# Spreading 1/rms through DRAM instead of with selector matmuls, in an attention and channel-mix kernel

The change replaces, for batches 3 to 7, the matmuls that spread the reciprocal rms over the partitions by a write to DRAM and a broadcast read. With it comes a new order of every instruction, made so that transposes and loads are apart in time, and finer stores at the end.

## Chip, cores and metric

One core of a Trainium2 chip. The metric is device time in microseconds (us) of one execution, lower is better. A profile is one execution seen by the hardware profiler; its span, from first to last instruction, is 1.7 to 2.5 us shorter than the time of that run. Engines are named as the profile names them: PE (TensorE), PEld (its weight loads), DVE (VectorE), ACT (ScalarE), POOL (GpSimd), SP (SyncE). "SPq" and "ACTq" are those two engines' sequencers, where transfers are issued.

## The reference, cut to what matters

```python
# q, k, v: (8 batches, 8 heads, 576 rows, 64) float32
kv  = einsum('bhsd,bhse->bhde', k, v)
out = einsum('bhsd,bhde->bhse', q, kv)
rms = sqrt(mean(out * out, axis=-1, keepdims=True) + 1e-06)
x   = out / rms * g_norm                      # then heads side by side: (8, 576, 512)

x_prev = x shifted by one row, zero first
xk = mu_k * x + (1 - mu_k) * x_prev
xr = mu_r * x + (1 - mu_r) * x_prev
k  = maximum(xk @ w_k, 0)                     # 512 -> 1024
r  = sigmoid(xr @ w_r)                        # 512 -> 512
result = r * ((k * k) @ w_v)                  # 1024 -> 512
```

The attention part goes by batch (576 rows), the mix by groups of 512 rows: nine groups, 0 to 8. A group needs `x` of one or two batches; group 3 is the first that needs batch 3, group 4 needs 3 and 4, group 5 needs 5 after the end of 4.

## The kernel before

The program is a set of pieces, each for one engine, and a hand-made list `ORDER` that says in which order all pieces are emitted. Each engine runs its own instructions strictly in that order. An entry is `name:engine:slots`; a slot is a buffer of the kind that the piece claims. PSUM is the kind `ps` with only four slots (2 x 512 float32 on each partition), and a piece that claims a slot waits until the last user of that slot is done.

Names, with batch `b` or group `g`: `load_*` loads (issued by POOL); `qTd` transpose by DMA (issued by SP); `kv`, `u` the two attention products on small PE tiles; `kvc`, `uc` their copies out of PSUM; `sq` squares; `st` sum of squares on PE; `rs` the reciprocal square root on ACT; `sp` its spread by PE; `x` the multiply; `d` difference to the row before; `tk`, `tr`, `xk`, `xr` the blends; `K`, `relu`, `sqk`, `R`, `sig`, `V`, `o` the mix; `S` its stores, issued by SP.

The step that the change replaces, for batches 1 to 7. `rs` has one row per head pair and head in use, so each row has to be spread over 64 partitions:

```python
st = add(f"st{b}", {"PE": 0.25}, st_mm, deps=sqs + [p_ones], bufs=[pst, sq], mode=3)
rp = add(f"rs{b}", {"ACT": 0.54}, st_rs, deps=[st], bufs=[pst, rs], mode="norm")
for half in range(2):
    pp = [Buf("ps") for _ in range(2)]                       # two PSUM slots

    def sp_mm(_, half, pp):                                  # line 530 is its matmul
        for hp in range(NHP):
            nc.tensor.matmul(get(pp[hp // 2])[:, hp % 2, 0:HS], sel[32 * hp:32 * hp + 32].rearrange("p e d -> p (e d)"),
                             get(rs)[32 * hp:32 * hp + 32, HS * half:HS * half + HS], start=True, stop=True)

    def x_mul(_, half, i, ps):                               # line 535; g_norm is inside sel
        c = HS * half
        nc.vector.tensor_tensor(out=get(xT)[:, 2 * i:2 * i + 2, NP + c:NP + c + HS],
                                in0=flat(slice(2 * i, 2 * i + 2))[:, :, c:c + HS], in1=get(ps)[:, :, 0:HS], op=ALU.mult)
# ... cut ...
```

The stores, in pieces that follow the layout of the output (one piece may be two or more transfers):

```python
def store(eng, g, ci, ot, cs):
    row = 0
    while row < 128:
        # ... cut: the next run of rows that lie together ...
        (nc.sync if eng == "SP" else nc.scalar).dma_start(out=dst, in_=ot[row:row + cnt, cs])
        row += cnt
```

The order around batch 3, cut to it (`st3` to its first blend):

```
st3::3 rs3::0 kvc4.0.0:D:0 kvc4.0.2:D kvc4.0.1:D R2.0::2 relu2.1::1 sp3.0::03 load_q6.0::1 sqk2.3 R2.1 R2.3::1
x3.0.1::1 x3.0.0 sqk2.1 sig2.0::1 sp3.1::30 S1.0 x3.1.0 R2.2 sig2.1::2 x3.1.1 d3.0::0 d3.2 S0.0 tk3.2:D:0 xk3.2
```

## Time and profile before

| | before |
|---|---|
| time, median of 3 runs | 210.9 us (210.78 to 212.5) |
| span of the profiled run | 207.6 us |
| PE, DVE, ACT busy | 94%, 68%, 59% |
| first R, first K (the start of its weight load; its first matmul is 0.2 us later) | 19.3 us, 24.5 us |
| first K to the end of the last matmul | 176.4 us |
| last matmul to the end | 6.7 us |

Below are the head of the profile page and its rows for PE and for the clock. The rows cut the span into 40 slices of 5.2 us; a digit is the busy share in tenths, in the row PEclk the granted TensorE clock in tenths of full speed.

```profile
span 207.6 us, 3798 instructions
## 1 busy us (share of the span) xinstructions
PE 195.7 (94%) x1526; PEld 93.9 (45%) x1526; DVE 141.1 (68%) x262; ACT 122.0 (59%) x146; POOL 28.7 (14%) x45
## 2 busy tenths in 40 slices
PE   7598999999999999999999999999999999999970
...
PEclk9955999999999999999999999999999999999998
```

PE is full from the fifth slice to the last but two: this kernel is bound by PE's work, but for its start (half clock in two slices) and its tail. The chain that ended last, by engine, says the same:

```profile
PE 88%; DMA 3%; ACT 2%; POOL 2%; DVE 1%; issue 1%; POOLq 0%
```

The timeline around batch 3 shows the spread. Columns: start in us, duration, engine, line, operation, output and input, count, and in brackets the idle time before it and what ended it.

```profile
75.04 0.65 ACT L519 ACTIVATE rs<-ps 128x576 bf16<-128x576 f32 x1 [0.33 <-PE ps L514]
...
75.89 0.30 PE L530 MATMUL ps<-rs,sel 32*128 32x288 bf16 x4
...
76.31 1.42 DVE L535 TENSOR_TENSOR xT<-uT,ps 128x576 bf16<-128x576 bf16 x2 [0.26 <-PE ps L530]
77.02 8.22 SPq L389 DMA_TRANSPOSE qT<-q  x1
```

From the end of `rs` (75.69) to the first multiply (76.31) it takes 0.6 us. The price is PE: a selector step takes 0.234 us in the chain of waits, plus about 0.1 us to switch to small tiles and back, and the two PSUM slots. The last line is the other thing that the change is after: a transpose whose issue holds SP's sequencer for 8.22 us beside loads.

### The profile page before, as it was taken

How to read it: one execution, taken by the hardware profiler on the slowest of the kernel's cores; microseconds unless marked ns; L12 is line 12 of the kernel's file. 1: busy time of each engine (PE TensorE's matmuls, PEld its weight loads, DVE VectorE, ACT ScalarE, POOL GpSimd, SP SyncE). 2: the span in 40 equal slices, each digit the busy share in tenths (PEclk: the TensorE clock that was granted, in tenths of full speed). 3: DMA queues.
4: the chain of work that ended last, by engine and by line, in shares of the span. 5: the costliest groups of instructions: out<-in, count | busy, mean ns of one | idle time of the engine just before them, and what ended most of it. 6: DMA issues, size and time to landing. Idle time of an engine off the chain costs nothing.

```text
span 207.6 us, 3798 instructions
## 1 busy us (share of the span) xinstructions
PE 195.7 (94%) x1526; PEld 93.9 (45%) x1526; DVE 141.1 (68%) x262; ACT 122.0 (59%) x146; POOL 28.7 (14%) x45
## 2 busy tenths in 40 slices
PE   7598999999999999999999999999999999999970
PEld 6443455444344534444854544444344444444440
DVE  1268728996788899998577997896848736322420
ACT  4567768287928798838956368456884045471010
POOL 7893301033000340001020000000000000000000
PEclk9955999999999999999999999999999999999998
DMA  6999999999999999999999348403200003603185
GB/s 156 188 200 204 204 203 206 203 149 183 182 145 191 213 277 231 163 191 266 113 160 213 88 107 196 117 0 82 73 0 0 0 3 93 214 0 91 42 232 144
DMA packets 39301, 29.71 MB, mean 143 GB/s; under 512 B 13548, under 2 KB 34804, under 8 KB 39284
## 3 DMA queue, kind: packets, MB, share of 16 engines
q0 software_dynamic: 21232, 16.48, 52.9%
q1 hardware_dynamic: 17516, 12.43, 28.3%
q10 hardware_dynamic: 536, 0.56, 0.9%
q8 instruction: 12, 0.20, 0.4%
q14 instruction: 5, 0.04, 0.1%
HBM read 33.56 MB, written 9.44 MB: 207 GB/s over the span
## 4 chain that ended last, share of the span: by engine, by line
PE 88%; DMA 3%; ACT 2%; POOL 2%; DVE 1%; issue 1%; POOLq 0%
PE ps L655 31%; PE ps L599 30%; PE ps L621 16%; DMA v<-in_v_dram 3%; PE ps L348 3%; PE ps L431 2%; PE ps L363 2%; PE ps L530 2%; POOL q L276 1%; PE ps L514 1%; PE ps L425 1%; PE ps L476 1%; ACT relu L603 1%; ACT L200 1%; DVE xr L566 0%
## 5 line engine op out<-in xcount | busy, mean ns | idle before, releaser
L599 PE MATMUL ps<-xk,w_k 128*128 128x512 bf16 (+1 forms) x320 | 67.4, 358 | 0.0
L655 PE MATMUL ps<-w_v,sqk 128*128 128x512 bf16 (+1 forms) x296 | 66.6, 374 | 0.0
L603 ACT ACTIVATE relu<-ps 128x1024 bf16<-128x1024 f32 x36 | 36.6, 1023 | 25.4 <-PE ps L599 23.5
L599 PEld LDWEIGHTS <-w_k 128*128 128x128 bf16 x320 | 30.1, 98 | 29.9 <-issue 1.6
L655 PEld LDWEIGHTS <-sqk 128*128 128x128 bf16 x296 | 27.6, 98 | 31.9 <-issue 1.1
L606 DVE TENSOR_TENSOR sqk<-relu 128x1024 bf16<-128x1024 bf16 x36 | 24.5, 687 | 21.2 <-ACT relu L603 21.1
L621 PE MATMUL ps<-w_r,xr 128*128 128x512 bf16 x144 | 35.5, 389 | 0.1
L659 DVE TENSOR_TENSOR out<-ps,sig 128x1024 f32<-128x1024 f32 (+2 forms) x21 | 22.3, 1069 | 11.5 <-PE ps L655 9.0
L626 ACT ACTIVATE sig<-ps 128x1024 bf16<-128x1024 f32 x18 | 18.1, 1022 | 16.8 <-PE ps L621 16.7
L535 DVE TENSOR_TENSOR xT<-uT,ps 128x576 bf16<-128x576 bf16 x28 | 20.1, 751 | 6.4 <-PE ps L530 6.4
L186 ACT ACTIVATE t<-d,mu_sb 128x576 bf16<-128x576 bf16 x23 | 16.4, 767 | 13.1 <-DVE d L556 13.1
L621 PEld LDWEIGHTS <-xr 128*128 128x128 bf16 x144 | 13.7, 100 | 17.8 <-issue 1.8
L276 POOL DMA_DIRECT2D q<-in_q_dram x12 | 8.6, 720 | 60.4 <-DMA qT<-q 39.2
L188 DVE TENSOR_SCALAR t<-d,mu_sb 128x576 bf16<-128x576 bf16 x41 | 13.5, 372 | 0.2
L180 ACT CAST uT<-ps 128x576 bf16<-128x576 f32 x16 | 9.9, 640 | 6.2 <-PE ps L431 5.3
L556 DVE TENSOR_TENSOR d<-xT 128x1152 bf16<-128x1152 bf16 (+1 forms) x18 | 12.4, 692 | 0.6
L182 DVE CAST uT<-ps 128x576 bf16<-128x576 f32 x12 | 9.1, 755 | 5.0 <-PE ps L425 3.8
L566 DVE TENSOR_TENSOR xr<-t,xT 128x1152 bf16<-128x1152 bf16 (+1 forms) x18 | 12.3, 687 | 0.2
L566 DVE TENSOR_TENSOR xk<-t,xT 128x1152 bf16<-128x1152 bf16 (+1 forms) x18 | 11.8, 687 | 0.3 <-ACT t L186 0.2
L276 POOL DMA_DIRECT2D k<-in_k_dram x11 | 7.9, 715 | 12.8 <-PE ps L348 10.7
L200 ACT ACT_TABLE_LOAD x7 | 9.0, 1283 | 0.8 <-PEq L719 0.7
L626 ACT ACT_TABLE_LOAD x7 | 9.0, 1283 | 0.1
(60 smaller groups left out, 125.1 us busy)
## 6 DMA issues: line engine op xcount, KB each, us to landing
out_dram<-out SPq DMA_DIRECT2D x23, 192.0 KB
q<-in_q_dram POOLq DMA_DIRECT2D x6, 576.0 KB, 14.2
v<-in_v_dram POOLq DMA_DIRECT2D x6, 576.0 KB, 15.6
k<-in_k_dram POOLq DMA_DIRECT2D x6, 576.0 KB, 17.4
out_dram<-out SPq DMA_DIRECT2D x24, 128.0 KB
out_dram<-out SPq DMA_DIRECT2D x23, 64.0 KB
w_k<-in_moe_w_k_dram POOLq DMA_DIRECT2D x2, 512.0 KB, 11.7
w_v<-in_moe_w_v_dram POOLq DMA_DIRECT2D x2, 512.0 KB, 17.0
```

The source lines that it names most:

```text
L186: nc.scalar.mul(out=dst, in_=src, mul=by)
L188: nc.vector.tensor_scalar_mul(out=dst, in0=src, scalar1=by)
L276: nc.gpsimd.dma_start(out=get(kvq[(n, b)])[:, h0:h1, :], in_=rows(n, b, h0, h1))
L535: nc.vector.tensor_tensor(out=get(xT)[:, 2 * i:2 * i + 2, NP + c:NP + c + HS], in0=flat(slice(2 * i, 2 * i + 2))[:, :, c:c + HS], in1=get( ...
L566: nc.vector.tensor_tensor(out=dst[:, hsl, c0:c0 + S], in0=get(t[key])[:, hsl, :], in1=get(xT)[:, hsl, 0:S], op=ALU.add)
L599: nc.tensor.matmul(get(ps)[:, fc % 2, a0:a1], w_k_sb[:, cc, 128 * fc:128 * fc + 128], xk[:, cc, x0:x0 + a1 - a0], start=(cc == 0), stop=(c ...
L603: nc.scalar.activation(out=get(rt), in_=get(ps), func=AF.Relu)
L606: nc.vector.tensor_mul(out=get(sqk)[:, 2 * f2:2 * f2 + 2, :], in0=get(rt), in1=get(rt))
L621: nc.tensor.matmul(get(ps)[:, ci % 2, :], xr[:, cc, c:c + 128], w_r_sb[:, cc, :], start=(cc == 0), stop=(cc == NHP - 1))
L626: nc.scalar.activation(out=get(sg), in_=get(ps), func=AF.Sigmoid)
L655: nc.tensor.matmul(get(ps)[:, ci % 2, cs], get(sqk)[:, fc, 128 * ci:128 * ci + 128], w_v_sb[:, fc, cs], start=(fc == 0), stop=(fc == NFC - 1))
L659: nc.vector.tensor_mul(out=get(ot)[:, xs, cs], in0=get(ps)[:, xs, cs], in1=get(sg)[:, xs, cs])
```

## The change

Intent: take ten selector steps off the full PE (batches 3 to 7, two each) and let DMA do the spread; keep transposes and loads apart in time; let the order hold even if late loads take a third longer; shorten the tail with stores from two issuers.

```diff
+    SPREAD = 3
+    scratch = {b: dram.tile([H, S], BF16, name=f"scratch{b}") for b in range(SPREAD, B)}
...
+            if b >= SPREAD:
+                rows8 = scratch[b]
+
+                def rs_out(eng, rs=rs, rows8=rows8):
+                    (nc.sync if eng == "SP" else nc.scalar).dma_start(out=rows8, in_=get(rs)[0:128:16, :])
+
+                def rs_in(eng, rows8=rows8):
+                    for e in range(2):
+                        (nc.sync if eng == "SP" else nc.scalar).dma_start(
+                            out=get(sq)[64 * e:64 * e + 64], in_=rows8.rearrange("(h e) s -> e h s", e=2)[e:e + 1].broadcast_to([64, NHP, S]))
+
+                def x_stt(_, i):
+                    hsl = slice(2 * i, 2 * i + 2)
+                    nc.vector.scalar_tensor_tensor(out=get(xT)[:, hsl, NP:NP + S], in0=flat(hsl), scalar=g_col, in1=get(sq)[:, hsl],
+                                                   op0=ALU.mult, op1=ALU.mult)
+
+                wr = add(f"rw{b}", {"SP": 0.5, "ACT": 0.45}, rs_out, deps=[rp], bufs=[rs], land=0.08)
+                rd = add(f"rr{b}", {"SP": 1.05, "ACT": 0.9}, rs_in, deps=[wr], bufs=[sq], land=1.6)
...                  (two x pieces for the batch instead of four)
-            for half in range(2):
+            for half in range(2 if b < SPREAD else 0):
...                  (last two groups: one piece for each store transfer, on SP or ACT)
-                    on = {"SP": 0.45 * stores(g, ci)}
-                    if g == NG - 1:
-                        on["ACT"] = 0.45 * stores(g, ci)
+                    for i, part in enumerate([rows] if g < NG - 2 else [[r] for r in rows]):
+                        on = {"SP": 0.53 * len(part)}
+                        if g >= NG - 2:
+                            on["ACT"] = 0.45
```

`rw` is the write, `rr` the two broadcast reads. `w_r` is loaded in two pieces. The whole `ORDER` is new: much of batch 1 and 0.9 MB more of loads now come before the first K. Around batches 3 and 5 it reads (cut; batch 3's trip is issued by ACT, the others by SP):

```diff
+    st3::2 rs3::1 rw3:A load_q5.0::1 sqk2.0::0 xr2.2 kv4.0::1 kvc4.0.2:D:0 sqk2.1 kvc4.0.1:D kvc4.0.0:D K2.6 relu2.3::1
+    rr3:A K2.5 V2.3a::2 relu2.2::0 sqk2.2 sqk2.3 x3.0::1 R2.2::1 R2.3 V2.0a::0 R2.1::3 V2.2a R2.0 sig2.1::1 sig2.0::2
+    V2.0b V2.1a qTd4::1 u4.0::1 u4.1::3 V2.3b V2.2b d3.0::0 tk3.0:A:0 x3.1 d3.2 xk3.0 tk3.2:D uc4.1:A:0 uc4.0:A u4.2::3
+    u4.3::1 S1.3 S1.2 S0.1 S0.3 S0.0 xk3.2 V2.1b uc4.2:A uc4.3:A sq4.0:D:0 o2.1::0 K3.4::3 K3.5
...
+    st5::2 rs5::1 K4.1 ... rw5:S rr5:S x5.1::1 d5.2::0 S1.0 S3.0 S1.1 x5.0 d5.0 S2.3 load_v6.0::0 load_k6.0::0 ...
+    tr5.2:A:0 tk5.2:A:1 ... kv6.0::0 V4.3a V4.1b kvc6.0.2:A:0 kvc6.0.1:A kvc6.0.0:A u6.0::0
```

## The prediction

> **What bounds the kernel now.** TensorE (PE). The busy table gives it 195.7 of 207.6 us; the list of its instructions in time order shows no gap from 37 us to its last matmul at 200.96 us; the chain of waits is 88% PE. Group starts in that list: four 512-column matmuls take 0.863 us (1.68 at half clock); a switch to small tiles (kv, u, st, sp) and back costs about 0.1 us more. DVE (68%) and ACT (59%) are off the path. Three parts are not PE-bound:
> - Start. The software-queue loads run back to back; 6.46 MB, through the second half of w_v, took until 36.6 us (0.193 MB/us; data was used about 1.2 us after its last packet). Blended inputs gate the first R at 19.3 us; the first K starts at 24.75.
> - Clock. The windows show 0.63 and 0.50 granted at 10 to 20 us. The Trainium skill, "TensorE: Matmul & The Clock Gate", Part 1, says an idle window of about 3.4 us halves the clock; this trace agrees (drop at 11.3 us, return at 21.5).
> - Tail. 6.6 us from last matmul to end; SP issues its last store at 203.9.
>
> **PE work.** For batches 3 to 7 ten selector broadcasts go: 0.234 us each plus about 0.1 of mode switch, 3.4 us. Summing the measured steps over the new order gives 169.2 us from the first K to the last matmul. The old order has 176.2, so 7 us less follow K: 3.4 removed, the rest mostly batch-1 work moved before it.
>
> **Start.** The new load order puts 3.77 MB (w_r included) ahead of w_k0 instead of 2.88. At the measured rate w_k0 lands near 27.2 us, and DVE's queue (x0.3, d0.3, blends) ends about then. So the first K is at 27.5 to 29: about 3.5 us given back. w_v0, w_v1 and batch 2's k, v land just when needed.
>
> **Round trip.** Four PSUM multiplies of 0.75 us per batch become two scalar_tensor_tensor, estimated at 1.27 us (1152 elements at the rate of the fp32-PSUM operations): DVE saves 0.5 us a batch, off the path. The norm chain grows: write and read each pay a DMA latency; "DMA: Bandwidth & Descriptors", Anatomy, puts the fixed part at about 2 us, of which the 1.2 us above is what this trace shows. I estimate 6 to 8 us from rs to the broadcast, against 1 now. The new order leaves 14 to 17 us of PE work between st and the first K that needs the batch; I need 14 to 16. Batches 3 and 6 are tightest: about 1 us of PE stall in all, perhaps 3.
>
> **Transposes** took 8.2 to 12.4 us beside loads, 3.0 alone. Shortening them frees SP, off the PE path.
>
> **Tail.** Stores split over two issuers: about 5 us instead of 6.6.
>
> **Sum.** 28.2 + 169.2 + 1 + 5.1 = 203.5 us span, 4.1 less than 207.6; so about 206.7 us, range 204 to 210. Faster by over 2%: 0.47; within 2%: 0.49; slower: 0.04.
>
> **Right if** the profile shows the first K at 27.5 to 29 us, about 169 us from it to the last matmul plus at most 2 us of gaps, no selector broadcasts after batch 2, DVE under 70%, and a tail near 5 us.
>
> **Wrong if** the broadcast read (128 partitions reading eight rows) takes over 5 us beside loads, so that K of batches 3 or 6 waits; if the clock stays at half into the R matmuls (1 to 2 us more); if late loads delay w_v or batch 2; or if the start overlaps better than I think (2 us less).

## The result, and the profile after

The result is correct and slower: 225.92 us, median of three runs (225.07 to 227.47), against 210.9. The ratio is 1.070, with a 95% interval of 1.058 to 1.082. Ratios here are the mean time of one kernel's runs over that of the other's runs of the same rounds, so they are not quite the ratios of the medians quoted. Executions over 1.5% slower than the fastest of the same kernel are left out of the means.

| profiled run, us | before | predicted | after |
|---|---|---|---|
| first K | 24.5 | 28.2 (27.5 to 29) | 31.4 |
| first K to last matmul, sum of the steps | 174.5 | 169.2 | 169.2 |
| the same, measured | 176.4 | 170.2 | 189.5 |
| so lost in waits and at half clock | 1.9 | 1 (perhaps 3) | 20.3 |
| tail | 6.7 | 5.1 | 4.7 |
| span | 207.6 | 203.5 | 225.7 |

"Sum of the steps" adds, over the order of PE, what each step takes where PE does not wait and the clock is full, for example 0.863 us for four 512-column matmuls. The head of the page, the rows of PE and clock, and the chain:

```profile
span 225.7 us, 3739 instructions
## 1 busy us (share of the span) xinstructions
PE 200.9 (89%) x1482; PEld 100.5 (45%) x1502; DVE 139.7 (62%) x249; ACT 121.5 (54%) x149; POOL 29.7 (13%) x46
## 2 busy tenths in 40 slices
PE   7597999999999955939999998499999999999991
...
PEclk9855699999999997967999999979999999999998
```

```profile
PE 57%; DMA 14%; DVE 10%; ACT 3%; SPq 3%; issue 2%; ACTq 0%; DVEq 0%
PE ps L629 22%; PE ps L685 18%; PE ps L651 9%; DMA sq<-scratch 8%; DMA scratch<-rs 3%; DMA out_dram<-out 2%; DVE xT L543 2%; DVE d L584 2%; PE ps L436 2%; SPq L615 2%; PE ps L735 1%; DVE t L192 1%; PE ps L368 1%; DVE out L689 1%; DVE xT L56
```

PE has three holes, in slices 15 and 16 (79 to 90 us), 18 (96 to 102 us) and 25, 26 (135 to 147 us), and the clock falls behind each. The chain, 88% PE before, now goes 14% through DMA: the broadcast read (`sq<-scratch`), the write (`scratch<-rs`) and a store. PE's busy sum is higher although its work is less: at half clock a matmul counts about double (four of 512 columns take 1.68 us instead of 0.863), and the half clock lasted 32 us of the span, before 12.

The timeline around batch 3, to be held against that of before (lines that are not about the trip are left out):

```profile
76.24 0.65 ACT L524 ACTIVATE rs<-ps 128x576 bf16<-128x576 f32 x1 [0.33 <-PE ps L519]
...
76.92 0.66 ACTq L534 DMA_DIRECT2D scratch<-rs  x1
...
77.36 3.54 SPq L394 DMA_TRANSPOSE qT<-q  x1
...
80.30 5.67 ACTq L538 DMA_DIRECT2D sq<-scratch  x2
81.00 6.35 SPq L615 DMA_DIRECT2D out_dram<-out  x10
...
86.08 1.02 ACT L633 ACTIVATE relu<-ps 128x1024 bf16<-128x1024 f32 x1 [6.98 <-DMA out_dram<-out]
...
87.15 1.45 PE L651 MATMUL ps<-w_r,xr 128*128 128x512 bf16 x4 [4.80 <-ACT relu L633]
...
94.95 1.42 DVE L543 SCALAR_TENSOR_TENSOR xT<-uT,mu_sb,sq 128x1152 bf16<-128x1152 bf16 x1 [6.53 <-DMA sq<-scratch]
```

The transpose holds SP for a short time now, 3.54 us: that intention is met (the five of them held it for 21.3 us, before 42.4). But from the end of `rs` (76.89) to the first multiply it is 18.1 us, against 0.6 before. And look at what ACT did: from 80.3 to 86.1 it did nothing but issue two reads, and it stood for about 4.4 us between them. What it stood for is in the chain, here in order of time (start, us, what):

```profile
79.10 1.80 SPq L394
...
81.00 0.56 SPq L615
...
81.61 3.73 DMA out_dram<-out
85.36 9.56 DMA sq<-scratch
...
94.95 1.43 DVE xT L543
```

ACT's second read starts at 85.36, the moment at which a store that SP had issued at 81.61 landed. The two have no data in common. In the built program and in the trace's semaphore events, the transfers of SP and of ACT take turns on eight completion counters (this is how the program is built), and the read's counter was the one that this store still held: it received the store's last update at 85.34. Behind ACT's blocked read stood a relu whose PSUM slot PE needed: PE's first hole. Then the read itself took 9.56 us beside the other stores and two loads (it is not small: the profile lists 288 KB for each of the two reads of a batch, which the prediction does not mention); DVE, in order, did nothing else meanwhile, ACT's next piece needed DVE's difference, and behind it stood the copy that frees a PSUM slot: PE's second hole. These waits, in the profile's list (engine, line, releaser: us in total, times, longest):

```profile
DVE xT L543 <- DMA sq<-scratch: 13.0, 5, 6.5
...
ACT relu L633 <- DMA out_dram<-out: 7.0, 1, 7.0
...
PE ps L651 <- ACT relu L633: 4.8, 1, 4.8
PE ps L436 <- ACT uT L184: 3.9, 1, 3.9
PE ps L436 <- ACT kv L184: 3.9, 2, 3.7
```

The last line is batch 5. Its chain in order of time:

```profile
126.46 0.66 ACT rs L524
127.14 4.58 DMA scratch<-rs
...
132.50 5.16 DMA sq<-scratch
```

The write of 9 KB took 4.58 us beside the loads of batches 6 and 7, the read 5.16: 10.6 us from `rs` to the multiply at 137.76. `x5` late made `d5` late, so ACT's blends of batch 5 stood, and behind them in ACT's order stood the `kvc6` copies that PE's `u6.0` needed (3.7 us of PE).

Where no load was running, the trip was short. Batch 7, from the timeline:

```profile
170.43 0.65 ACT L524 ACTIVATE rs<-ps 128x576 bf16<-128x576 f32 x1
171.10 0.60 SPq L534 DMA_DIRECT2D scratch<-rs  x1
...
172.86 1.26 SPq L538 DMA_DIRECT2D sq<-scratch  x2
...
178.30 2.75 DVE L543 SCALAR_TENSOR_TENSOR xT<-uT,mu_sb,sq 128x1152 bf16<-128x1152 bf16 x2 [0.97 <-DMA sq<-scratch]
```

That is 7.2 us from the end of `rs` (171.08); the five trips took 18.1, 7.0, 10.6, 7.0 and 7.2 us.

### The profile page after: what moved, and what is told of

The parts are those of the page before. It is cut to its first block, busy times and chain, and to the rows that moved or that the text cites. A ratio compares the mean times of both kernels' runs of the same rounds, so it can differ in the third digit from the quotient of the medians.

```text
span 225.7 us, 3739 instructions
## 1 busy us (share of the span) xinstructions
PE 200.9 (89%) x1482; PEld 100.5 (45%) x1502; DVE 139.7 (62%) x249; ACT 121.5 (54%) x149; POOL 29.7 (13%) x46
## 4 chain that ended last, share of the span: by engine, by line
PE 57%; DMA 14%; DVE 10%; ACT 3%; SPq 3%; issue 2%; ACTq 0%; DVEq 0%
PE ps L629 22%; PE ps L685 18%; PE ps L651 9%; DMA sq<-scratch 8%; DMA scratch<-rs 3%; DMA out_dram<-out 2%; DVE xT L543 2%; DVE d L584 2%; PE ps L436 2%; SPq L615 2%; PE ps L735 1%; DVE t L192 1%; PE ps L368 1%; DVE out L689 1%; DVE xT L563 1%
## 5 line engine op out<-in xcount | busy, mean ns | idle before, releaser
L685 PE MATMUL ps<-w_v,sqk 128*128 128x512 bf16 (+1 forms) x288 | 68.5, 384 | 0.8 <-issue 0.6
L633 ACT ACTIVATE relu<-ps 128x1024 bf16<-128x1024 f32 x36 | 35.9, 1022 | 26.6 <-PE ps L629 13.9
L629 PEld LDWEIGHTS <-w_k 128*128 128x128 bf16 x320 | 30.9, 100 | 32.7 <-issue 5.5
L636 DVE TENSOR_TENSOR sqk<-relu 128x1024 bf16<-128x1024 bf16 x36 | 24.3, 687 | 28.9 <-ACT relu L633 28.8
L651 PE MATMUL ps<-w_r,xr 128*128 128x512 bf16 x138 | 34.8, 387 | 5.2 <-ACT relu L633 4.8
L190 ACT ACTIVATE t<-d,mu_sb 128x576 bf16<-128x576 bf16 x24 | 17.3, 770 | 21.6 <-DVE d L584 21.6
L656 ACT ACTIVATE sig<-ps 128x1024 bf16<-128x1024 f32 x18 | 17.9, 1022 | 15.2 <-DMA out_dram<-out 7.6
L651 PEld LDWEIGHTS <-xr 128*128 128x128 bf16 x144 | 14.0, 99 | 21.3 <-issue 6.2
L543 DVE SCALAR_TENSOR_TENSOR xT<-uT,mu_sb,sq 128x1152 bf16<-128x1152 bf16 x10 | 13.9, 1414 | 13.0 <-DMA sq<-scratch 13.0
L184 ACT CAST uT<-ps 128x576 bf16<-128x576 f32 x18 | 11.0, 637 | 5.6 <-PE ps L436 5.6
L436 PE MATMUL ps<-qT,kv 64*64 64x288 bf16 x96 | 6.3, 320 | 8.3 <-ACT uT L184 3.9
L280 POOL DMA_DIRECT2D v<-in_v_dram x11 | 7.9, 721 | 36.2 <-PE ps L353 35.1
L735 PE MATMUL ps<-zeros 128*128 128x224 bf16 x44 | 8.4, 380 | 1.2 <-DVE zeros L231 1.2
```

The lines of the kernel that those rows point to most:

```text
L190: nc.scalar.mul(out=dst, in_=src, mul=by)
L280: nc.gpsimd.dma_start(out=get(kvq[(n, b)])[:, h0:h1, :], in_=rows(n, b, h0, h1))
L543: nc.vector.scalar_tensor_tensor(out=get(xT)[:, hsl, NP:NP + S], in0=flat(hsl), scalar=g_col, in1=get(sq)[:, hsl], op0=ALU.mult, op1=ALU.mult)
L629: nc.tensor.matmul(get(ps)[:, fc % 2, a0:a1], w_k_sb[:, cc, 128 * fc:128 * fc + 128], xk[:, cc, x0:x0 + a1 - a0], start=(cc == 0), stop=(c ...
L633: nc.scalar.activation(out=get(rt), in_=get(ps), func=AF.Relu)
L636: nc.vector.tensor_mul(out=get(sqk)[:, 2 * f2:2 * f2 + 2, :], in0=get(rt), in1=get(rt))
```

## The experiments

Theories, with the letters that the texts use. A: the loss is the round trip where other transfers run, above all batch 3's, whose issues stand in ACT's order behind SP's stores. B: the trip is too long for this order wherever it is put, and loads whichever engine carries it; mending one place moves the loss to the next. C: the new order of loads and stores costs by itself, trip or no trip. D is about the late start: the half clock before the first K; D1 says that the dummy matmuls at the start pay for themselves and no more.

Unless said otherwise a run gave the right result, in three rounds beside the kernel before, whose medians were 210.5 to 211.0. "Lost" is, as in the table above, measured time from the first K to the last matmul less the sum of the steps; it includes half clock behind a wait. By stretches of PE's order, worked out from each profile (us; the columns end where V2, K3, R4, K5 and K6 begin, and at the last matmul):

```
                  to V2  V2-K3  K3-R4  R4-K5  K5-K6  K6-end
after               0.5   11.8    1.9    4.8    0.7    0.4
e1_sp               0.5    2.0    5.3    5.1    0.9    0.4
e2_stores_early     0.5    4.5    1.2    4.3    0.5    0.3
f1_mended           0.5    4.4    5.9    1.1    0.0    1.0
h1_no_latency       0.5    6.7    0.3    1.1    0.0    0.1
h2_no_transfer      0.5    0.0    0.1   -0.1    0.0    0.1
m1_late_only        0.5    2.6    3.1   -0.1    0.0    0.5
```

### e1_sp: batch 3's trip on SP instead of ACT

```diff
-rw3:A ... rr3:A
+rw3:S ... rr3:S
```

> Edit: batch 3's two round-trip transfers (rs to DRAM, DRAM to the broadcast) are issued from SP instead of ACT; nothing else. Theory A (a blocked in-order issuer): in the changed kernel ACT stood still from 80.3 to 86.1 us because its second broadcast read waited for a completion counter that an SP store was still holding; with SP issuing, relu and sigmoid go on, PE's gap of 5.1 us between R2.1 and V2.2a falls below 0.5 us, the broadcast lands by 86 us instead of 94.9, and the first K of group 3 starts at 90 to 93 us instead of 101.6. Span 214 to 218 instead of 225.7. Theory B (the transfer itself is slow beside loads, whoever issues it): the broadcast still lands after 91 us, the first K of group 3 starts after 97 us, span over 220.

220.25 us, ratio 1.045 (1.040 to 1.049); span 218.9. The hole at R2.1 is gone and `x3` starts at 84.99 instead of 94.95. So ACT's blocked issue was the first hole; the broadcast before 86 us and the first K of group 3, at 90.9, are where A had them. But the sum was 14.6 us lost, and the span lay just above the range that A gave: the trip of batch 4 now met loads (its write took 4.5 us), and 5.3 us went between K3 and R4, where 1.9 had gone. From the timeline of this run:

```profile
76.00 0.68 SPq L532 DMA_DIRECT2D scratch<-rs  x1
78.71 1.34 SPq L536 DMA_DIRECT2D sq<-scratch  x2
80.16 4.77 SPq L392 DMA_TRANSPOSE qT<-q  x1
84.97 5.07 SPq L613 DMA_DIRECT2D out_dram<-out  x9
84.99 1.42 DVE L541 SCALAR_TENSOR_TENSOR xT<-uT,mu_sb,sq 128x1152 bf16<-128x1152 bf16 x1 [4.57 <-DMA sq<-scratch]
```

Even unblocked, the trip is 9 us here (76.0 to 84.99) and holds DVE for 4.57; and the transpose behind it starts at 80.16 instead of 77.36.

### e2_stores_early: ten stores moved ahead of the trip

```diff
-u4.3::1 S1.3 S1.2 S0.1 S0.3 S0.0 xk3.2
+u4.3::1 xk3.2
+S0.1 S0.3 S0.0      (behind o0.1)
+S1.3 S1.2           (behind o1.1)
```

> Edit: ACT still issues batch 3's round trip; the five output stores of groups 0 and 1 that SP issued right beside it (81 to 87 us, 0.64 MB) are moved earlier in SP's order, to where their data is ready. So neither a store's counter nor store traffic stands before the second read. Theory A: ACT is held only until the write has landed (about 1.5 us), PE's 5.1 us gap between R2.1 and V2.2a falls below 1 us, the broadcast lands near 84 to 87 us, span 213 to 218. Theory B (loads slow the transfer): the broadcast lands after 90 us in spite of it and the span stays over 220.

217.97 us, ratio 1.032 (1.026 to 1.037); span 216.0. Better by 8 us than the kernel after, but the hole at R2.1 was 2.7 us, not under 1 (the broadcast, at 87.0, landed where A had it): ACT stood still, now until 81.36, when the write, its packets beside loads, had landed. So moving the stores freed the counter and not the order: the reads cannot be issued before the write has landed, and ACT can do nothing else in that time.

### e3_selector: selectors again for all batches, in the new order

```diff
-SPREAD = 3
+SPREAD = 8
-rw{b} rr{b} x{b}.0 x{b}.1                          (b = 3 to 7)
+sp{b}.0::.. x{b}.0.1 x{b}.0.0 ... sp{b}.1::.. x{b}.1.1 x{b}.1.0
```

> Edit: new order, loads, stores and tail, but batches 3 to 7 spread 1/rms as before (selector matmuls into PSUM, four multiplies); the round trip is gone. If the round trip is what costs (A or B): PE runs without gaps over 1 us after the first K (31.4 us), 169.2 plus 3.4 us of PE work, tail 4.8, so a span of 209 to 212, 14 to 17 us less than the changed kernel and 1 to 2% slower than before because of the later start. Theory C (the loads and stores reordered are themselves the cause, for instance the late k5, q7, v6, k6): gaps of several us remain near 82 to 100 and 139 to 145 us and the span stays over 216.

233.45 us, ratio 1.106 (1.101 to 1.110). The profiled run was slow, so its span (234.0) is not compared. A miss, and of my making: the selectors need two PSUM slots each, which the new order has handed to other pieces, and where I put them PE waited for slots (2.4 us ahead of K3.2, 1.8 to 2.0 us at each of three more places). As a test of C it says nothing. It shows only that the old spread does not fit this order in the places where I put it.

### e4_warm: more dummy matmuls against the half clock

```diff
-idle:28:0
+idle:48:0             (and 56 more dummies ahead of eight waits of the start)
```

> Edit: dummy matmuls are added in PE's waits of the first 19 us (48 instead of 28 at the start, then 4 to 8 before eight waits), nothing else. The changed kernel's PE clock was at half from 9.1 to 26.2 us and its first K came at 31.4 us, 3 us later than I predicted. Theory D (half clock): with the clock kept up the first K comes at 28.5 to 29.8 us and the span falls by about 2 us. Theory E (loads or DVE and ACT set the start): the first K stays at 31 us or later.

229.96 us, ratio 1.088 (1.081 to 1.096). The half clock of the start shrank to 11.0 to 17.9 us, and the first K still came later, at 35.92: PE does its dummies in order, and so many stood in front of real work. The size was badly chosen; as a remedy it is refuted at this size, and a smaller one was not tried.

### e5_noidle: the two later dummy groups taken out

```diff
-idle:6:3 ... idle:10:3
```

> Edit: the 6 and the 10 dummy matmuls that the change put just before the first R are taken out of the changed kernel; nothing else. In its trace they held PE for 1.5 and 1.9 us at half clock, between ss0.2 and ss0.3, on the way to the first K at 31.4 us. If they only delay the chain (theory D2): the first K comes 2 to 3 us earlier, at 28.5 to 29.5 us, and the span falls by as much. If they pay for themselves by bringing the full clock back earlier (theory D1): the clock stays at half into the R matmuls, the first K is at 31 us or later.

224.59 us (219.52 to 227.33), runs of both states, so no ratio. The profiled run, a slow one, has its first K at 30.93, with two stretches of half clock before it. In that run the clock was at half until 28.2 us, into the R matmuls that began at 26.2, as D1 says. But one run, of which there is no profile, took 219.52 us, 5.6 less than the fastest of the kernel after. One run decides nothing: whether the edit gains stays open here, and only f2 below speaks for D1.

### f1_mended and f2_mended_noidle: the edits of e1 and e2 together, and batch 6 ahead of batch 5's trip

```diff
 (the edits of e1_sp and e2_stores_early)
-kvc5.0.1:D:1
+kvc5.0.1:A:1
+load_v6.0::0 load_k6.0::0      (ahead of load_q7.0)
+kv6.0::0 kvc6.0.2:A:0 kvc6.0.1:A kvc6.0.0:A      (behind K4.6, ahead of x5)
```

> Edit: batch 3's round trip on SP, stores of groups 0 and 1 early (the two edits above together), batch 5's third kv copy on ACT so that it no longer stands behind batch 4's x on DVE, batch 6's kv product and copies ahead of batch 5's x and t on ACT and DVE, and batch 6's k and v loaded ahead of q7. Theory A (in-order engines blocked behind the round trip): PE's gaps at V3.2b to u5.1 (3.6 us on SP issue) and V4.1b to u6.0 (3.5 us) fall below 0.7 us each, PE's excess over the summed steps from the first K on falls from 14.6 us to below 5, span 206 to 211. Theory B (the round trip, 7 us quiet and 10 beside loads, is longer than the work the order leaves): gaps of the same size move to the first K of groups 4, 5 or 6, span over 214.

219.03 us, ratio 1.036 (1.029 to 1.043); span 217.2. Expected were 206 to 211. The hole ahead of `u6.0` is gone as planned (R4 to K5 lost 1.1 instead of 4.8), but in its place PE waited 2.6 us for the transpose of batch 4, which is now issued behind the reads on SP, and 3.1 us at `u5.3` behind a late `x4`, whose trip now met the loads I had moved. This is what B says: the trip is longer than the order has room for, and each edit moved the wait to the next engine in order.

f2_mended_noidle is the same without the two dummy groups:

> The mended kernel without the 6 and 10 dummies. If both theories hold (A and D2): 2 us under the mended kernel, span 204 to 209, about level with the kernel before or up to 1.5% better. If D1 holds, no faster than the mended kernel.

219.72 us, ratio 1.043 (1.038 to 1.048), first K at 31.55 and half clock until 29.0 us: no faster than f1, as D1 says.

### h1_no_latency and h2_no_transfer: the trip's issue and traffic without its wait, and no trip at all

Their outputs are wrong, which doesn't matter for the times. In h1 the transfers stay, but the broadcast lands in a tile that nobody reads, and the multiply takes the squares that are in `sq`. In h2 the two functions that issue the transfers do nothing.

```diff
 h1
-                            out=get(sq)[64 * e:64 * e + 64], in_=rows8...
+                            out=dummy[64 * e:64 * e + 64], in_=rows8...
 h2
-                    (nc.sync if eng == "SP" else nc.scalar).dma_start(out=rows8, in_=get(rs)[0:128:16, :])
+                    pass
-                    for e in range(2):
-                        (nc.sync if eng == "SP" else nc.scalar).dma_start(out=get(sq)[64 * e:64 * e + 64], in_=rows8...)
+                    pass
```

> Wrong results on purpose. Edit: all ten transfers of the round trip stay, issued from the same engines at the same places, but the broadcast lands in a tile that nobody reads, and the multiply takes the squares instead. So issue, blocking of ACT and SP, and traffic stay; only the wait of DVE for the data is gone. If the latency of the data is most of the loss: PE's excess over the summed steps after the first K (20.3 us in the changed kernel) falls below 8, mostly what ACT's standstill near 80 us costs (5 to 7 us), span 210 to 214. If blocked issuers are most of it: the excess stays above 12, span over 217.

> Wrong results on purpose. Edit: the round trip's transfers are not made at all; the multiply takes the squares. What is left is the change's order, loads, stores and start, with the best that a round trip could ever give. If the round trip is the cause (A or B): the excess after the first K is below 3 us, first K at 28 to 31.5 us, span 203 to 208, level with the kernel before or a little better. If the loads and stores of the new order are a cause of their own (theory C): the excess stays above 5 us, with gaps where q4, k5 or v6 and k6 come late.

h1: 213.96 us, ratio 1.017 (1.011 to 1.023); span 211.6. h2: 206.42 us, ratio 0.980 (0.975 to 0.985); span 203.8, first K at 28.89, 170.2 us from it to the last matmul, tail 4.7.

This settles it. Without the transfers the new order runs as its steps say, with 1 us lost in all (of which 0.5 at a place that every variant has), so C falls: after the first K the new order of loads, transposes, batch 1 and stores costs nothing by itself (the later start was foreseen). It is the trip: 225.9 less 206.4, or 19.5 us. Of that, 213.96 less 206.42, 7.5 us, is there although DVE does not wait for the data; the other 12.0 us goes with that wait. (The kernel after ran in another call than these two; the kernel before differed by 0.4 us between the two.) These differences of medians also hold differences of the start, before any trip: the first K of the profiled runs is at 31.4, 28.6 (h1) and 28.9 us (h2). From there to the last matmul they took 189.5, 178.3 and 170.2 us, so the trip costs 19.4 us, of which 8.1 without DVE's wait and 11.3 with it. (By the steps h1 lost 9.1 us; expected was under 8.) h1's timeline shows what most of the 8.1 us is (6.7 of it are lost between V2 and K3), the same block of ACT behind a store as in the kernel after:

```profile
77.66 5.58 ACTq L537 DMA_DIRECT2D dummy<-scratch  x2
78.29 6.43 SPq L614 DMA_DIRECT2D out_dram<-out  x10
...
83.35 1.02 ACT L632 ACTIVATE relu<-ps 128x1024 bf16<-128x1024 f32 x1 [7.05 <-DMA out_dram<-out]
84.39 1.28 ACT L655 ACT_TABLE_LOAD   x1
84.42 1.54 PE L650 MATMUL ps<-w_r,xr 128*128 128x512 bf16 x4 [4.87 <-ACT relu L632]
```

In h2 the same R2.1 runs without a break, at 79.66 (the same columns):

```profile
78.79 1.03 PE L681 MATMUL ps<-w_v,sqk 128*128 128x512 bf16 x4
...
79.66 1.03 PE L647 MATMUL ps<-w_r,xr 128*128 128x512 bf16 x4
```

### g1_tail and g2_tail: only the split stores, on the kernel before

g1 takes the kernel before and gives it the split stores of the last two groups, on SP and ACT (with the last stores in a somewhat different order); g2 also moves the last R matmuls and two stores earlier.

```diff
+                    for i, part in enumerate([rows] if g < NG - 2 else [[r] for r in rows]):      (g1, as in the change)
-V7.0a V7.0b V8.2a::1 R8.2::2 R8.3 V8.2b        (g2)
+R8.2::2 R8.3 sig8.1::2 V7.0a V7.0b V8.2a::1 V8.2b
```

> Edit: the kernel before with the change's store code alone: the stores of the last two groups split by row runs and shared between SP and ACT; order otherwise that of before. The tail from the last matmul to the end was 6.6 us before and 4.8 in the changed kernel: I expect 4.6 to 5.2 here, PE's stream unchanged, span 205.8 to 206.6, 0.5 to 0.9% faster. If the tail is not shortened, the gain in the changed kernel came from its order.

> Edit: the kernel before with the change's split stores, as in the first tail run, and in addition the last R pair and its sigmoid ahead of the last V of group 7, and two stores of group 6 brought forward, so that the end is not a burst (there SP and ACT still waited for completion counters and the last store went out at 206.0 us, 2.3 us after the last matmul). Expected tail 4.6 to 5.2 us instead of 6.7, ratio to before 0.990 to 0.996, unclear at best by the 2% rule. If the tail stays at 5.8 or more, the store burst is bound by its traffic and not by who issues it.

g1: 210.24 us, ratio 0.994 (0.986 to 1.002); tail 5.85 instead of 6.66. g2, in five rounds: 209.85 us, ratio 0.995 (0.991 to 1.000); tail 5.93. So the split stores give about 0.8 us of tail here, less than the 1.5 that I expected, and moving the last work earlier gives no more. The rest of the change's shorter tail (4.7) comes with its own order of the last two groups; which part of that order does it I did not try.

### m1_late_only: the trip only for batches 6 and 7

```diff
-SPREAD = 3
+SPREAD = 6
-rw{b} rr{b} x{b}.0 x{b}.1                                     (b = 3, 4, 5)
+sp3.0::30 x3.0.1::1 x3.0.0   (ahead of R2.2)     sp3.1::31 ... (ahead of V2.0b)
+sp4.0::20 ...                (ahead of R3.2)     sp4.1::13 ... (ahead of V3.0a)
+sp5.0::10 ...                (ahead of K4.5)     sp5.1::20 ... (ahead of K4.6)
```

> The order, loads, split stores and start of the kernel after; the DRAM round trip only for batches 6 and 7, whose trips run after the last loads and measured 7.0 and 7.2 us; batches 3, 4 and 5 take the selector matmuls of the kernel before again, placed where two PSUM slots are free (six selectors, about 2 us of PE with their mode switches). The kernel without any transfer measured 206.4. If the loss is the transfers beside loads (batches 3 to 5) and the quiet trips fit into the order's slack: 207.5 to 210.5 us, from the first K to the last matmul 171 to 174 us with the first K at 28 to 31 depending on the half-clock windows, and no PE gap over 1.5 us after V5. If the quiet trips cost too, by their issues and broadcasts alone: gaps around K6 and K7 and over 212 us. My placement of the selectors could cost 1 to 2 us by itself through PSUM slots, as it did in the selector run before.

215.67 us in five rounds, ratio 1.024 (1.018 to 1.030); span 213.2. Not the 207.5 to 210.5 that I hoped for (and 178.3 us from the first K to the last matmul, not 171 to 174), so no version that beats the kernel before came out. The table of losses says where it went: 5.7 us between V2 and R4, mostly at my selectors (PE idle for 1.3 us ahead of K4.5, where the selector waited behind a relu for its slots; 1.1 ahead of V2.0b; 0.8 ahead of K4.7), and a tail of 6.3 us, which I did not look into. From R4 on, with the two quiet trips of 7.0 and 7.3 us in it, PE lost 0.4 us. That half of the expectation was met: a quiet trip fits into this order's slack and costs PE nothing.

## Why the prediction was wrong

The prediction was 206.7 us, with 204 to 210 as its range and 4% for slower by over 2%. Measured: 225.9.

1. **What failed: the term "about 1 us of PE stall in all, perhaps 3".** It stood on "I estimate 6 to 8 us from rs to the broadcast" against "14 to 17 us of PE work between st and the first K". The 6 to 8 us is right for a quiet chip: 7.0, 7.0 and 7.2 us for batches 4, 6 and 7. It is wrong beside other transfers: 18.1 us for batch 3 and 10.6 for batch 5. Stall and half clock came to 20.3 us. I had named this ("if the broadcast read ... takes over 5 us beside loads") and given it almost no weight; and the tight batch besides 3 was 5, not 6.
2. **What the step left out altogether: the trip's issues stand in an engine's order.** I counted the trip as latency in the norm chain, with the issuing engine free. h1 shows 8.1 us of loss after the first K although DVE does not wait for the data: ACT stood 4.3 us between two reads (4.4 in the kernel after), because a completion counter was held by a store of SP's, and PE stood behind ACT for a PSUM slot. The Trainium skill, "DMA: Bandwidth & Descriptors", section "Anatomy of one DMA", says that a wait on a semaphore happens on the issuing sequencer before dispatch; this trace agrees (ACT's reads at 80.30 and 85.36, its relu at 86.08). I had read that page for its fixed cost of about 2 us, and not for this.
3. **The fixed cost of a transfer was too small under load.** The quiet write took 1.8 us from its issue to the read's issue (batch 7), near the about 2 us in that section, which the page fits to transfers issued by POOL, while these are issued by SP; beside loads 4.6 us (batch 5). The same page, section "Latency and other measured facts", gives the latency of HBM as 0.2 us on average and 2 us at high load. The direction agrees with these runs; 4.6 us for 9 KB is more than its figures would have led me to.
4. **The wait spreads in in-order engines.** With 14 us of slack between `st3` and K3, an 18 us trip should cost some 4 us by this estimate; the stretch lost 11.8, because PE stood twice before K3, for PSUM slots that ACT frees in an order with the trip's work ahead. Slack has to be counted at the next instruction of each engine in the trip's path (ACT's relu, DVE's next piece), not only at the K that uses the data. e1, e2 and f1 show it from the other side: each removed or shortened the hole it aimed at, and got 6 to 8 us of 19.5.
5. **The start was mis-sized, by 3 us.** Predicted 27.5 to 29 us, measured 31.4. The load pace was as predicted (w_k0 had its last packet at 26.2 us and landed at 27.8; I had it landing near 27.2). What moved was the half clock: until 26.2 us in the profiled run, instead of 21.5 before. In the other runs with this same start (e1, e2, e3, f1, h1, h2, m1) it ended between 16.5 and 23.4 us and the first K came at 28.3 to 30.5, so 28.2 was the best of a range. The start of the kernel before varies as well: in g1 and g2, which have it, the half clock ended at 25.4 and 23.6 us and the first K came at 27.2 and 25.7, not 24.5. The lengths (6.8, 10.2, 13.7 and 17.1 us) are near multiples of 3.41 us, as the Trainium skill, "TensorE: Matmul & The Clock Gate", Part 1, has it for a window that runs freely; the runs agree, and show two to five such windows in a row. That an idle window brings the half clock, for which the prediction cites this page, these traces do not show: in the 3.4 us before the drop PE was busy for 2.4 us in the kernel before and 0.8 in the kernel after. Why the same start draws two windows once and five another time stays open. In the prediction this was a risk ("1 to 2 us more"); it was 3.
6. **What was right.** Work after the first K: h2 measured 170.2 us where 169.2 plus about 1 was predicted, and its span of 203.8 is close to the predicted 203.5. (The prediction set 169.2 against 176.2, the old stretch as measured from its first K matmul. The old steps sum to 174.5, so 5.3 us of steps went, not 7.) So the gain was there: without the transfers the change is 2% faster. No selector matmul runs after batch 2; DVE is at 62%; the tail is 4.7 us (about 5). The new multiply took 1.414 us each, not the 1.27 estimated; it is off the path.

The expected gain of 4 us is there (h2), and the trip that was to bring it cost 19.4. In the original kernel the selector costs PE about 0.33 us a step, and it answers in 0.6 us on engines whose order the kernel controls.

## What to carry to other kernels

In this kernel a transfer in the middle of a dependency chain cost more than its latency: it stopped the in-order engine that issues it until every semaphore and counter it needed was free, and the trip took 7 us quiet but 9 to 18 us beside loads and stores. Before moving a broadcast off a full engine, find for each engine on the new path the next instruction that others wait for, and count the slack there. And when a change of many parts goes wrong, take the suspected part's transfers away while keeping the order (a wrong result): one such run told more here than the attempts to mend it.

## What the Trainium skill lacked or had wrong

- "DMA: Bandwidth & Descriptors", "Issuing engines are not separate DMA queues", says that issuing from several engines only saves the usually small time to initiate a transfer. The runs show that who issues can matter more than that (e1, with one trip moved from ACT to SP, is 5.7 us faster than the kernel after): this program lets SP's and ACT's transfers share eight completion counters, and a read on ACT waited from about 81 to 85.36 us for a store of SP's; with the read on SP (e1) that hole was gone. No page says that a transfer can wait for another issuer's unrelated one.
- The same page has no figure for a small transfer beside loads: a 9 KB write took 1.8 us quiet and 4.6 us beside loads; the trip of write and broadcast read 7.0 to 7.2 us quiet, and 9 to 18 us beside loads and stores.
- The same page gives no time for a transpose by DMA beside loads: here its issue held SP's sequencer for 8.2 to 12.4 us in the kernel before, 3.0 us alone; 3.0 to 7.6 us in the new order.
- No page that I found gives the time of a scalar_tensor_tensor: 1.414 us for 128x1152 bf16, where a tensor_tensor of 128x576 with one operand in PSUM takes 0.751.
- "TensorE: Matmul & The Clock Gate", Part 1: the window of 3.41 us agrees, and the page does say that the slow start varies from run to run with the phase of the window. That runs with the same start spend two windows in a row at half clock (h1, to 16.5 us) or five (the kernel after, to 26.2 us), and that the first K moves by 3 us with it, is not there.
